# Retention and low-rank mixer on one core: batch 1's u by token and through DMA, transposing DMAs on two queues, two loads and one chunk moved

## The chip, the cores and the metric

The kernel runs on one core of a Trainium2 chip. The metric is the device time of one execution in microseconds. The kernel before takes 226.94 us (median of 3 runs, 226.93 to 226.95).

The core has five engines, each with one instruction stream that it works through in order: TensorE (PE) for matrix products into PSUM, VectorE (DVE) and ScalarE (ACT) for elementwise work and for reading PSUM, GpSimd (POOL), and SyncE (SP), which here does nothing but issue DMAs. Engines and DMAs are ordered among each other by semaphores: an instruction may wait until a semaphore has reached a count, and raises one when it is done.

## The reference

Four batches of 768 tokens; 8 heads of 64 channels make 512 channels per token.

```python
gamma = 1.0 - 2.0 ** (-5.0 - np.arange(H))
for t in range(S):                                   # retention, per batch and head
    state = gamma * state + outer(k[t], v[t])
    x[t] = (q[t] @ state) / sqrt(D)
h = x.transpose(0, 2, 1) @ U @ V                     # low rank over tokens, rank 32
u = x + h.transpose(0, 2, 1)
out = u + np.maximum(u @ w_ch1, 0.0) @ w_ch2         # 512 -> 2048 -> 512
```

## The kernel before

A batch is cut into six chunks of 128 tokens. For each chunk, POOL scales k and q by powers of gamma (`ret_k`, `ret_q` in `ret_in`, line 268, giving `kd` and `qd` in bf16), ACT casts v (`ret_v`), and then:

- `ret_T` (line 415) turns `qd` and `kd` so that channels lie on partitions. For batch 1 PE does it and DVE or ACT copies the result out of PSUM; from batch 2 on (`by_dma`) two transposing DMAs do it (`ret_T_dma`, line 277): **Tq** for q, **Tk** for k.
- `ret_S` forms the scores of a chunk, and DVE masks them (tile `a`).
- `ret_O` adds the part of the old state and the part of the scores, ACT copies the sum out of PSUM (tile `x`), and DVE masks the new state (tile `state`). The state of chunk c is read by `ret_O` of chunk c + 1.

Then `mix_P` (line 486) forms the rank-32 product P from all six x, and u comes from it in one of two ways. By channel (`mix_u`): PE turns x by products with the identity, adds V times P, and ACT or DVE copies a quarter of u, turned, out of PSUM into `uT`. By token (`mix_n`, line 526): PE forms the low-rank part of one chunk of 128 tokens, DVE adds x into `res`, ACT casts that back to bf16 into `xs`, and a transposing DMA writes it to `uT`. The six of a batch are called **T0 to T5** here. Where u was made by token, the second layer's last addition uses `res`; where not, `mlp2` adds one more product of V and P per chunk. `by_token` (line 518) says which chunks go which way: before, chunks 3 to 5 of batch 1 and all of batches 2 and 3.

The first layer, **MLP1**, has 32 blocks of work per batch (`mlp1`: 16 groups of 128 hidden channels, two halves of 384 tokens, four matmuls each). Half 0 reads chunks 0 to 2 of `uT`, half 1 chunks 3 to 5. For b > 0 the order is eight blocks of half 0, eight of half 1, then in turn. Each block fills a PSUM bank that `evict` (line 118) empties through a relu into `gT`. `evict` picks ACT or DVE by a planner's account of each engine's booked time (`Balance`, `bal.book`), when the program is built. In MLP1 of batches 1 and 2 three banks take turns (`set_banks([0, 1, 2])`, line 712), in batch 3 six. The second layer, **MLP2**, has 48 slots of two matmuls (128x512), eight per chunk of 128 tokens.

The order around this work is written out by slot: `weave` (line 590) runs the slots of MLP1 and MLP2 of batch b (0 to 31, then n1 = 32 and up) and puts the retention and the mixing of batch b + 1 between them, where the tables `at` (ret_T), `S_at`, `O_at` and `mix_at` say. So slot 10 of batch 1's MLP1 is where chunk 0 of batch 2 is turned.

All DMAs of q, k, v and out, and all transposing DMAs, are issued by SP, in the program's order. Each raises one of eight semaphores when it lands (DMAHW0 to DMAHW7 below), taken in turn over all DMAs of SP and ACT, and waits first for the earlier DMA on the same one.

Of the kernel before, what the change touches and what calls it, by code (L numbers as in the profile page):

```python
# [47 lines left out]
def kernel(  # L48
# [19 lines left out]
    NCB = DM // P  # L68
# [5 lines left out]
    bal = Balance()  # L74
# [31 lines left out]
    def mm_bank(who="main"):  # L106
        if use[who] is None:
            who = "main"
        b = use[who][n_use[who] % len(use[who])]
        n_use[who] += 1  # L110
        taken[b] = n_bank[0]
        return bank(b)

    def matmul(o, l, r, cols, **kw):
        nc.tensor.matmul(o, l, r, **kw)  # L115
        bal.mm(cols)
# [21 lines left out]
    def load_chunk(b, c, kinds="kqv"):  # L138
        t = staged.setdefault((b, c), {})
        for nm in kinds:  # L140
            load_one(t, b, c, {"k": k, "q": q, "v": v}[nm], nm + "_n")
# [26 lines left out]
    for what in ("q0", "kA", "q1", "k2", "k3", "vA", "q2", "k4", "v2", "k5", "v3", "v4", "v5"):  # L168
        src, i = {"q": q, "k": k, "v": v}[what[0]], what[1]
# [74 lines left out]
    xs, rc = {}, {}  # L244
# [8 lines left out]
    def ret_q(b, c, eng):  # L253
        qd = rmid.tile([P, H, D], bf16, tag="qd", name=f"qd_{b}_{c}", bufs=4)
        eng.tensor_tensor(qd, rc[b, c]["q_n"], Gq[:, c].unsqueeze(2).to_broadcast([P, H, D]),  # L255
                          op=ALU.mult)
        rc[b, c]["qd"] = qd
# [5 lines left out]
        rc[b, c]["vb"] = vb  # L263


    EARLY = (2, 3, 4)

    def ret_in(b, c):
        ret_k(b, c, nc.gpsimd)
        ret_q(b, c, nc.gpsimd)  # L270
        if b == 1 and c in EARLY:
            load_chunk(b + 1, c - EARLY[0])

# [3 lines left out]
    def ret_T_dma(b, c):  # L277
        r = rc[b, c]
        qkT = rmid.tile([P, 2, NP, P], bf16, tag="qkT", name=f"qkT_{b}_{c}", bufs=6)
        for i, src in ((0, r["qd"]), (1, r["kd"])):  # L280
            nc.sync.dma_start_transpose(out=qkT[:, i], in_=src.rearrange("p h d -> p (h d)"))
            r["qk"[i] + "T"] = qkT[:, i]


# [2 lines left out]
    G, V, A = nc.gpsimd, nc.vector, nc.scalar  # L287
# [196 lines left out]
    uTs, gTs, Ps = {}, {}, {}  # L484
# [12 lines left out]
    def mix_x(b, hf, c, bk=None):  # L497
        pieces[b, hf, c] = piece = (mm_bank("mix") if bk is None else bank(bk))[:, :HS]
        for jj in range(HS // P):
            j = hf * (HS // P) + jj  # L500
            matmul(piece[:, ts(jj, P)], xs[b][:, j, ts(c, P)], ident, P, start=(jj == 0),
                   stop=False, skip_group_check=True)

    def mix_h(b, hf, c):
        piece = pieces.pop((b, hf, c))
        matmul(piece, Ps[b][:, ts(c, P)], Vb[:, ts(hf, HS)], HS, start=False, stop=True,
               skip_group_check=True)
        evict(uTs[b][:, c, ts(hf, HS)], piece, HS)
# [7 lines left out]
    res = {}  # L516

    def by_token(b, j):
        return b >= 2 or (b == 1 and j >= NCK // 2)

    def res_of(b):
        if b not in res:
# [3 lines left out]
    def mix_n(b, j):  # L526
        h = mm_bank("mix")
        matmul(h, Vb[:, ts(j, P)], Ps[b], DM, start=True, stop=True)
        u = res_of(b)[:, j]
        nc.vector.tensor_tensor(u, h, xs[b][:, j], op=ALU.add)  # L530
        bal.book("V", 0.69)
        nc.scalar.activation(xs[b][:, j], u, AF.Copy)  # L532
        bal.book("A", 0.63)
        nc.sync.dma_start_transpose(out=uTs[b][:, :, ts(j, P)], in_=xs[b][:, j])


    def mlp1(b, m, hf):
# [8 lines left out]
    def mlp1_two(b, ms, hf):  # L546
        if b not in gTs:
            gTs[b] = gtp.tile([P, NM, S], bf16, tag="gT", name=f"gT_{b}")
        g = [mm_bank()[:, :HS] for _ in ms]
        for cs in ((0, 1), (2, 3)):  # L550
            for m, o in zip(ms, g):
                for c in cs:
                    matmul(o, w1b[:, c, ts(m, P)], uTs[b][:, c, ts(hf, HS)], HS, start=(c == 0),
                           stop=(c == NCB - 1))
        for m, o in zip(ms, g):
            evict(gTs[b][:, m, ts(hf, HS)], o, HS, relu=True)
# [43 lines left out]
    def put(side, i, f):  # L600
        side.setdefault(int(i), []).append(f)
# [17 lines left out]
    def mix_side(b, i, side):  # L619
        put(side, i + 2, lambda: mix_P(b))  # L620
        js = [j for j in range(NCK) if by_token(b, j)]
        for n, j in enumerate(js):
            put(side, i + 5 + n, lambda j=j: mix_n(b, j))
        if b == 1:
            for c in range(NCB):
                put(side, i + 5 + len(js) + c, lambda c=c: mix_u(b, 0, c))
        return side


# [55 lines left out]
    for b in range(B):  # L685
        nxt = b + 1 < B
        slots = mlp1_slots(b)
        n1 = len(slots)
        side = {}
        set_banks([0, 1, 2, SA, SB, OB])  # L690
        if b == 0:
            taken.update({i: n for n, i in enumerate((1, 2, 0, OB, SA, SB, TP))})
            set_banks([1, 2, 0, OB, SA, SB, TP])
            slots[:4] = [lambda: mlp1_two(0, (0, 1), 0), lambda: None,
                         lambda: mlp1_two(0, (0, 1), 1), lambda: None]
            for i, s in ((1, 2), (2, 3)):
                put(side, i, lambda s=s: load_w1(512 * s, 512))
            for s in range(4):
                put(side, 4 + s, lambda s=s: load_w2(s))
            for c, nm in ((0, "kq"), (1, "kq"), (2, "kq"), (0, "v"), (3, "kq"), (1, "v"), (4, "kq"),  # L700
                          (2, "v"), (3, "v"), (5, "kq"), (4, "v"), (5, "v")):
                put(side, 14, lambda c=c, nm=nm: load_chunk(1, c, nm))
            at, lead, mix_at = [n1 + 7 + 5 * c for c in range(NCK)], 4, n1 + 38
            S_at = {(0, 1): n1 + 14, (2, 3): n1 + 24, (4,): n1 + 30, (5,): n1 + 35}
            O_at = [n1 + i for i in (19, 22, 29, 32, 35, 38)]
        if b:

            slots = slots[:16:2] + slots[1:16:2] + slots[16:]
        if b == 1:
            slots[:2] = [lambda: mlp1_two(1, (0, 1), 0), lambda: None]  # L710
        if b and nxt:
            set_banks([0, 1, 2])
            at, lead, mix_at = [10 + 4 * c for c in range(NCK)], 5, n1 + 25
            S_at = {(0, 1): 27, (2, 3): 37, (4, 5): 47}
            O_at = [32, 35, 43, 46, 53, 56]
        if nxt:
            ret_side(b + 1, at, lead, S_at, O_at, side)
            put(side, n1, lambda: set_banks([0, 1], [2]))
            put(side, mix_at, lambda: use.update(mix=[2, SA, SB, OB]))
            mix_side(b + 1, mix_at, side)  # L720
        if b in (1, 2):
            for c, i in ((3, 0), (4, 7), (5, 15)):
                put(side, i, lambda c=c: load_chunk(b + 1, c))
        weave(slots + mlp2_slots(b), side)

# [29 lines left out]
```

## Time and profile before

| | before |
|---|---|
| median of 3 runs | 226.94 us |
| the profiled execution | 226.93 us, of which the span from first to last instruction is 225.2 us |
| ACT busy | 112.0 us (50%), 220 instructions |
| DVE busy | 85.4 us (38%), 163 instructions |
| MLP1 of batch 1, 2, 3 starts on PE at | 81.52, 131.24, 180.31 us |
| MLP2 of batch 3 ends on PE at | 222.1 us |
| transposing DMAs | 24 for q and k, 15 for u, all issued by SP |
| granted TensorE clock | 1.000 |

The rows of the profile name an engine, a line of the kernel, an operation, what it writes and reads, and how many were merged. "SPq" is SP issuing. Matmuls overlap, so a matmul row lasts longer than the distance to the next one: 128x512 rows follow each other every 0.216 us, and the four of an MLP1 block take 0.65 us. Times are microseconds from the start of the span.

### The profile page before, as it was taken

To read this page: it belongs to the slowest core of one execution; us is meant where nothing else is said; L and a number is where in the kernel's file an instruction comes from. 1 tells how busy PE (TensorE), PEld (TensorE's weight loads), DVE (VectorE), ACT (ScalarE), POOL (GpSimd) and SP (SyncE) were. 2 spreads that over 40 slices of the span, in tenths; PEclk is the share of its full clock that TensorE was granted. 3 is DMA by queue.
4 is the path that set the end of the run, shared out by engine and by line. 5 is a ranking of instruction groups with operands and counts; after the bars stand their busy time and mean duration, and the time that the engine had idled before them with its cause. 6 is when DMAs were issued, how large, how long until landed. Compare 5 with 4: busy or idle time off the path is not lost.

```text
span 225.2 us, 4288 instructions
## 1 busy us (share of the span) xinstructions
PE 219.7 (98%) x1735; PEld 124.7 (55%) x1735; DVE 85.4 (38%) x163; ACT 112.0 (50%) x220; POOL 58.9 (26%) x66
## 2 busy tenths in 40 slices
PE   7998999999999999999999999999999999999994
PEld 2466655655656466556554456565554455654454
DVE  8597630003777450034673610045674410001221
ACT  3377657751355277767133547776323467760000
POOL 6756920046643431431035103330000000000000
PEclk9999999999999999999999999999999999999999
DMA  6998999999899999989499669995311580001212
GB/s 172 243 265 181 162 189 199 198 223 226 186 232 219 234 232 206 201 168 127 101 210 243 196 134 231 174 187 97 93 49 57 131 143 0 0 3 47 88 52 95
DMA packets 100772, 34.85 MB, mean 155 GB/s; under 512 B 87152, under 2 KB 97808, under 8 KB 100752
## 3 DMA queue, kind: packets, MB, share of 16 engines
q1 hardware_dynamic: 94640, 30.29, 66.0%
q0 software_dynamic: 6112, 4.29, 13.0%
q8 instruction: 13, 0.21, 0.4%
q14 instruction: 7, 0.06, 0.1%
HBM read 27.46 MB, written 6.29 MB: 150 GB/s over the span
## 4 chain that ended last, share of the span: by engine, by line
PE 90%; DMA 3%; POOL 2%; DVE 1%; ACT 1%; SPq 0%; issue 0%; ACTq 0%
PE bk L115 88%; DMA in<-in_q_dram 3%; POOL qd L304 1%; PE bk L418 1%; ACT st L292 1%; PE bk L311 1%; DVE a L345 1%; SPq L165 0%; POOL kd L299 0%; DVE kT L294 0%; PE bk L323 0%; DVE vb L294 0%; DVE res L575 0%; ACTq L292 0%
## 5 line engine op out<-in xcount | busy, mean ns | idle before, releaser
L115 PE MATMUL bk<-w2b,gT 128*128 128x512 bf16 (+2 forms) x416 | 92.0, 363 | 0.0
L115 PE MATMUL bk<-uT,w1b 128*128 128x384 bf16 x512 | 84.3, 326 | 0.0
L120 ACT ACTIVATE gT<-bk 128x384 bf16<-128x384 f32 x123 | 60.4, 491 | 31.8 <-PE bk L115 31.8
L115 PEld LDWEIGHTS <-w1b 128*128 128x128 bf16 x512 | 49.9, 98 | 33.3 <-issue 0.2
L115 PEld LDWEIGHTS <-gT 128*128 128x128 bf16 x416 | 37.9, 98 | 37.8 <-issue 0.8
L250 POOL TENSOR_TENSOR kd<-k_n,Gk 128x512 bf16<-128x512 f32 x18 | 18.8, 1042 | 77.8 <-DMA k_n<-in_k_dram 58.7
L440 DVE TENSOR_TENSOR a<-bk,mask 128x512 bf16<-128x512 f32 x36 | 22.4, 683 | 36.0 <-PE bk L115 35.8
L575 DVE TENSOR_TENSOR res<-bk,res 128x512 f32<-128x512 f32 (+2 forms) x17 | 10.6, 626 | 44.6 <-PE bk L115 44.6
L459 ACT ACTIVATE x<-bk 128x512 bf16<-128x512 f32 x18 | 10.7, 595 | 23.3 <-PE bk L115 23.3
L255 POOL TENSOR_TENSOR qd<-q_n,Gq 128x512 bf16<-128x512 f32 x18 | 18.8, 1042 | 6.8 <-DMA qkT<-qd 3.4
L478 DVE TENSOR_TENSOR state<-bk,bmask 128x512 bf16<-128x512 f32 x15 | 10.4, 691 | 10.7 <-PE bk L115 10.7
L261 ACT ACTIVATE vb<-v_n 128x512 bf16<-128x512 f32 x18 | 10.8, 622 | 5.8 <-DMA v_n<-in_v_dram 5.8
L530 DVE TENSOR_TENSOR res<-bk,x 128x512 f32<-128x512 f32 x15 | 9.7, 685 | 8.4 <-PE bk L115 8.4
L532 ACT ACTIVATE x<-res 128x512 bf16<-128x512 f32 x15 | 9.3, 630 | 7.1 <-DVE res L530 6.9
L115 PEld LDWEIGHTS <-qkT 64*128 64x128 bf16 (+1 forms) x204 | 8.4, 95 | 7.1 <-issue 3.2
L115 PE MATMUL bk<-idle 128*128 128x512 bf16 x29 | 10.3, 499 | 1.2 <-DVE idle L179 1.2
L124 DVE COPY qkT<-bk 128x1024 bf16<-128x1024 bf16 x3 | 2.1, 691 | 23.9 <-PE bk L418 23.9
L115 PE MATMUL bk<-vb,a 128*128 128x64 bf16 (+1 forms) x208 | 10.1, 193 | 0.0
L115 PE MATMUL bk<-P_sb,Vb 128*128 128x512 bf16 x24 | 9.1, 380 | 0.0
L115 PEld LDWEIGHTS <-a 128*128 128x128 bf16 (+1 forms) x208 | 8.5, 97 | 0.7
L115 PE MATMUL bk<-vb,kd 128*128 128x128 bf16 (+1 forms) x88 | 8.2, 219 | 0.2 <-DVE vb L294 0.2
L345 DVE TENSOR_TENSOR a<-bk,mask 128x512 bf16<-128x512 f32 x12 | 7.7, 684 | 1.4 <-PE bk L115 1.4
(85 smaller groups left out, 132.0 us busy)
## 6 DMA issues: line engine op xcount, KB each, us to landing
out_dram<-res SPq DMA_DIRECT2D x23, 256.0 KB, 2.4
k_n<-in_k_dram SPq DMA_DIRECT2D x22, 256.0 KB, 5.0
v_n<-in_v_dram SPq DMA_DIRECT2D x22, 256.0 KB, 5.0
q_n<-in_q_dram SPq DMA_DIRECT2D x18, 256.0 KB, 5.1
w2b<-in_moe_w_ch_dram POOLq DMA_DIRECT2D x4, 512.0 KB, 15.0
in<-in_q_dram SPq DMA_DIRECT2D x3, 512.0 KB, 6.3
w1b<-in_moe_w_ch_dram POOLq DMA_DIRECT2D x4, 256.0 KB, 6.0
w1b<-in_moe_w_ch_dram POOLq DMA_DIRECT2D x2, 512.0 KB, 9.2
```

Source lines behind the costliest of these rows:

```text
L115: nc.tensor.matmul(o, l, r, **kw)
L120: nc.scalar.activation(o, i, AF.Relu if relu else AF.Copy)
L250: eng.tensor_tensor(kd, k_n, Gk[:, c].unsqueeze(2).to_broadcast([P, H, D]), op=ALU.mult)
L255: eng.tensor_tensor(qd, rc[b, c]["q_n"], Gq[:, c].unsqueeze(2).to_broadcast([P, H, D]), op=ALU.mult)
L261: nc.scalar.activation(vb, rc[b, c]["v_n"], AF.Copy)
L345: nc.vector.tensor_tensor(r0["a", c][:, e], r0["s", c][e].rearrange("p (n t) -> p n t", n=NP), mask0[:, c].unsqueeze(1).to_broadcast([P, N ...
L440: nc.vector.tensor_tensor(r["a"][:, e], r["s"][e].rearrange("p (n t) -> p n t", n=NP), mask4, op=ALU.mult)
L459: nc.scalar.activation(xs[b][:, c], o, AF.Copy)
L478: nc.vector.tensor_tensor(sb, ps.rearrange("p (n t) -> p n t", n=NP), bmask4, op=ALU.mult)
L530: nc.vector.tensor_tensor(u, h, xs[b][:, j], op=ALU.add)
L532: nc.scalar.activation(xs[b][:, j], u, AF.Copy)
L575: nc.vector.tensor_tensor(o, chp.pop((b, j)), o if by_token(b, j) else xs[b][:, j, ds(lo, w)], op=ALU.add)
```

## The change

Four things are changed. Batch 1's u is made by token for all six chunks, so `mix_u` is no longer called after batch 0 and three V-times-P products leave `mlp2`. The transposing DMAs alternate between two queues: Tk and the odd ones of T0 to T5 are issued by ACT (`nc.scalar`), Tq and the even ones by SP; for Tk the planner books 1.25 us of ACT. Batch 1's chunk 5 is turned one slot earlier, its scores are formed one slot earlier, `ret_O` of chunks 4 and 5 comes one and two slots earlier, `mix_at` moves from n1 + 38 to n1 + 36, and the first `mix_n` from four to five slots after that to four. And the loads of batch 2's chunk 2 move from batch 0's MLP2 to slot 0 of batch 1's MLP1 (its chunk 3 then goes to slot 2).

```diff
-    EARLY = (2, 3, 4)
+    EARLY = (2, 3)
...
         for i, src in ((0, r["qd"]), (1, r["kd"])):
-            nc.sync.dma_start_transpose(out=qkT[:, i], in_=src.rearrange("p h d -> p (h d)"))
+            (nc.scalar if i else nc.sync).dma_start_transpose(out=qkT[:, i],
+                                                              in_=src.rearrange("p h d -> p (h d)"))
+            if i:
+                bal.book("A", 1.25)
...
     def by_token(b, j):
-        return b >= 2 or (b == 1 and j >= NCK // 2)
+        return b >= 1
...
-        nc.sync.dma_start_transpose(out=uTs[b][:, :, ts(j, P)], in_=xs[b][:, j])
+        (nc.scalar if j % 2 else nc.sync).dma_start_transpose(out=uTs[b][:, :, ts(j, P)], in_=xs[b][:, j])
...
-            put(side, i + 5 + n, lambda j=j: mix_n(b, j))
-        if b == 1:
-            for c in range(NCB):
-                put(side, i + 5 + len(js) + c, lambda c=c: mix_u(b, 0, c))
+            put(side, i + (4 if b == 1 else 5) + n, lambda j=j: mix_n(b, j))
...
-            at, lead, mix_at = [n1 + 7 + 5 * c for c in range(NCK)], 4, n1 + 38
-            S_at = {(0, 1): n1 + 14, (2, 3): n1 + 24, (4,): n1 + 30, (5,): n1 + 35}
-            O_at = [n1 + i for i in (19, 22, 29, 32, 35, 38)]
+            at, lead, mix_at = [n1 + i for i in (7, 12, 17, 22, 27, 31)], 4, n1 + 36
+            S_at = {(0, 1): n1 + 14, (2, 3): n1 + 24, (4,): n1 + 30, (5,): n1 + 34}
+            O_at = [n1 + i for i in (19, 22, 29, 32, 34, 36)]
...
-        if b == 1:
-            slots[:2] = [lambda: mlp1_two(1, (0, 1), 0), lambda: None]
...
-            for c, i in ((3, 0), (4, 7), (5, 15)):
+            for c, i in ((2, 0), (3, 2), (4, 7), (5, 15)) if b == 1 else ((3, 0), (4, 7), (5, 15)):
```

The first place where instructions move is SP's stream at the end of batch 0's MLP2, where u of batch 1 is turned. In the rows, `uT_1` and `x_1` are batch 1's, `out_0` and `res_0` batch 0's, and the brackets hold the semaphores that a row waits for. Before:

```order
L578 DMA out_0_dram<-res_0_901 128x512 [waits DMAHW4_49,DVE_49]
L534 DMA_TRANSPOSE uT_1_1288<-x_1_1008 128x4x128 [waits DMAHW5_49,PE_49,Activation_49]
L534 DMA_TRANSPOSE uT_1_1288<-x_1_1008 128x4x128 [waits DMAHW6_49,Activation_49]
L534 DMA_TRANSPOSE uT_1_1288<-x_1_1008 128x4x128 [waits DMAHW7_49,Activation_49]
L578 DMA out_0_dram<-res_0_901 128x512 [waits DMAHW0_49,DVE_49]
```

The three are T3, T4 and T5; each waits for its own semaphore's earlier DMA and for ACT's cast, and for no other transposing DMA. The same place of SP after the change:

```order
L581 DMA out_0_dram<-res_0_901 128x512 [waits DMAHW1_49,DVE_49]
L537 DMA_TRANSPOSE uT_1_1276<-x_1_1008 128x4x128 [waits DMAHW2_49,PE_49,Activation_49]
L537 DMA_TRANSPOSE uT_1_1276<-x_1_1008 128x4x128 [waits DMAHW4_49,DMAHW3_49,Activation_49]
L537 DMA_TRANSPOSE uT_1_1276<-x_1_1008 128x4x128 [waits DMAHW6_49,DMAHW5_49,Activation_49]
L581 DMA out_0_dram<-res_0_901 128x512 [waits DMAHW0_49,DVE_49]
```

These are T0, T2 and T4, on semaphores 2, 4 and 6. T2 and T4 each have one wait more: T2 for semaphore 3, T4 for semaphore 5. Those are the semaphores of T1 and T3, which ACT issues. ACT's stream at that place after the change, from the casts of `mix_n` to the first evictions of MLP1:

```order
L535 ACTIVATE x_1_1008<-res_1_1285 128x512 [waits DVE_49] x2
L537 DMA_TRANSPOSE uT_1_1276<-x_1_1008 128x4x128 [waits DMAHW3_49,DMAHW2_49,Activation_49]
L535 ACTIVATE x_1_1008<-res_1_1285 128x512 [waits DVE_49] x2
L537 DMA_TRANSPOSE uT_1_1276<-x_1_1008 128x4x128 [waits DMAHW5_49,DMAHW4_49,Activation_49]
L535 ACTIVATE x_1_1008<-res_1_1285 128x512 [waits DVE_49] x2
L537 DMA_TRANSPOSE uT_1_1276<-x_1_1008 128x4x128 [waits DMAHW7_49,DMAHW6_49,Activation_49]
L120 ACTIVATE gT_1_1340<-bk1_122_1341 128x384 [waits PE_49]
L120 ACTIVATE gT_1_1340<-bk0_123_1347 128x384 [waits PE_49]
L120 ACTIVATE gT_1_1340<-bk2_124_1359 128x384 [waits PE_49]
```

T1, T3 and T5 stand between ACT's casts and ahead of ACT's first ten evictions of MLP1. T1 waits for semaphore 2 (T0), T3 for 4 (T2), T5 for 6 (T4). Taken together with SP's rows, each of T1 to T5 waits until the one before it has landed. Batches 2 and 3 have the same rows at the same place.

The third place is ACT's stream in MLP1 of batch 1 from slot 9 on, where batch 2's q and k are turned (`qkT_2_0` is chunk 0 of batch 2). Before it held evictions alone:

```order
L120 ACTIVATE gT_1_1355<-bk1_132_1424 128x384 [waits PE_49]
L120 ACTIVATE gT_1_1355<-bk0_133_1433 128x384 [waits PE_49]
L120 ACTIVATE gT_1_1355<-bk2_134_1439 128x384 [waits PE_49]
L120 ACTIVATE gT_1_1355<-bk1_135_1445 128x384 [waits PE_49]
L120 ACTIVATE gT_1_1355<-bk0_136_1455 128x384 [waits PE_49]
```

And now:

```order
L120 ACTIVATE gT_1_1340<-bk1_131_1415 128x384 [waits PE_49]
L281 DMA_TRANSPOSE qkT_2_0_1421<-kd_2_0_1377 128x4x128 [waits Pool_49]
L120 ACTIVATE gT_1_1340<-bk1_134_1436 128x384 [waits PE_49]
L120 ACTIVATE gT_1_1340<-bk0_135_1446 128x384 [waits PE_49]
L281 DMA_TRANSPOSE qkT_2_1_1452<-kd_2_1_1411 128x4x128 [waits DMAHW4_49,DMAHW3_49,Pool_49]
L120 ACTIVATE gT_1_1340<-bk0_138_1473 128x384 [waits PE_49]
L120 ACTIVATE gT_1_1340<-bk2_139_1483 128x384 [waits PE_49]
L281 DMA_TRANSPOSE qkT_2_2_1489<-kd_2_2_1442 128x4x128 [waits DMAHW7_49,DMAHW5_49,Pool_49]
L120 ACTIVATE gT_1_1340<-bk2_142_1504 128x384 [waits PE_49]
L120 ACTIVATE gT_1_1340<-bk1_143_1514 128x384 [waits PE_49]
```

Tk of each chunk stands after two evictions; the two evictions in between (bk_132 and 133, 136 and 137 and so on) are DVE's now. Tk of chunk 1 waits for semaphore 3, which is SP's Tq of chunk 0, and Tk of chunk 2 for semaphore 5, Tq of chunk 1. SP's stream has the other half:

```order
L135 DMA v_n_2_4_1397<-in_v_dram 128x8x64 [waits DMAHW2_49]
L281 DMA_TRANSPOSE qkT_2_0_1421<-qd_2_0_1379 128x4x128 [waits DMAHW3_49,DMAHW6_49,PE_49,Pool_49]
L281 DMA_TRANSPOSE qkT_2_1_1452<-qd_2_1_1413 128x4x128 [waits DMAHW4_49,DMAHW5_49,PE_49,Pool_49]
L135 DMA k_n_2_5_1461<-in_k_dram 128x8x64
L135 DMA q_n_2_5_1463<-in_q_dram 128x8x64 [waits DMAHW0_49]
L135 DMA v_n_2_5_1465<-in_v_dram 128x8x64 [waits DMAHW1_49]
L281 DMA_TRANSPOSE qkT_2_2_1489<-qd_2_2_1444 128x4x128 [waits DMAHW2_49,DMAHW7_49,PE_49,Pool_49]
L281 DMA_TRANSPOSE qkT_2_3_1520<-qd_2_3_1481 128x4x128 [waits DMAHW3_49,PE_49,Pool_49]
```

Tq of chunks 0 and 1 wait for semaphores 6 and 4, ACT's Tk of the same chunk; Tq of chunks 2 and 3 for 7 and 3 likewise. Behind chunk 3 SP issues Tq of chunk 4 with no wait for ACT; Tk of chunk 4 then waits for Tq of chunks 3 and 4, in batch 2 Tq of chunk 5 waits for Tk of chunk 4 and Tk of chunk 5 for Tq of chunk 5. In batch 3 Tq of chunks 3, 4 and 5 stand in a row, Tk of chunk 4 waits for all three and Tk of chunk 5 for none of them.

## The prediction

> **What bounds the kernel now.** I read the page first, then the chain of waits in order of time, then who waited for whom.
>
> ```profile
> span 225.2 us, 4288 instructions
> PE 219.7 (98%) x1735; PEld 124.7 (55%) x1735; DVE 85.4 (38%) x163; ACT 112.0 (50%) x220; POOL 58.9 (26%) x66
> ...
> 69.41 152.68 PE bk L115 x1114
> ...
> ACT gT L120 <- PE bk L115: 31.8, 120, 4.4
> ```
>
> PE is the bound, and the third line says how tightly: the chain's last 152.68 us are 1114 matmuls with no wait among them. Every other engine waits for PE; ACT did so 120 times before an eviction of MLP1. So matmuls taken out are a gain at their full length, and each new wait of PE is a loss at its full length. ACT's half-empty row promises little: it evicts in order, and what stops it stops PE as soon as the three banks are full.
>
> **PE work.** The end of batch 0's MLP2, on PE and DVE, where batch 1's u is made:
>
> ```profile
> 71.53 0.40 PE L115 MATMUL bk<-qkT 64*128 64x128 bf16 x8
> ...
> 73.91 0.40 PE L115 MATMUL bk<-state,qkT 128*128 128x128 bf16 x4
> ...
> 75.87 0.39 PE L115 MATMUL bk<-P_sb,Vb 128*128 128x512 bf16 x1
> ...
> 77.61 0.59 PE L115 MATMUL bk<-w2b,gT 128*128 128x512 bf16 x2
> 78.04 0.38 PE L115 MATMUL bk<-P_sb,Vb 128*128 128x512 bf16 x1
> ...
> 79.34 0.33 PE L115 MATMUL bk<-ident,x 128*128 128x128 bf16 x3
> ...
> 81.52 10.73 PE L115 MATMUL bk<-uT,w1b 128*128 128x384 bf16 x65
> ...
> 71.97 1.29 DVE L440 TENSOR_TENSOR a<-bk,mask 128x512 bf16<-128x512 f32 x2 [1.15 <-PE bk L115]
> 73.17 0.68 DVE L478 TENSOR_TENSOR state<-bk,bmask 128x512 bf16<-128x512 f32 x1
> 75.51 0.69 DVE L575 TENSOR_TENSOR res<-bk,x 128x512 f32<-128x512 f32 x1 [1.66 <-PE bk L115]
> ```
>
> From 79.34 to 81.52 stand the four `mix_u` and two slots of MLP2 (0.43 each, 78.04 - 77.61): 2.18 - 0.87 = 1.30 us that leave. Three `mix_n` products come (3 x 0.216 = 0.65) and three products in batch 1's MLP2 go (0.65), so **PE gains 1.30 us**.
>
> Chunk 5 drawn together gives some of it back. The state of chunk 4 is ready at 73.85, 2.32 after the scores began (71.53), and its reader `ret_O` stood at 73.91, 0.06 later. Now four matmuls instead of six (0.43 less) stand between, so PE waits about **0.45**; the masks and the state keep their length. Without that wait the first `mix_n` would stand where 75.87 is; with it t0 = 76.3. From t0 PE has six `mix_n`, one V-times-P product and eight slots: 7 x 0.216 + 8 x 0.433 = 4.98, so it reaches MLP1 at 81.3, against 81.52.
>
> **The transposes of u.** This decides. One transposing DMA alone, all of u's, one with another close behind it, one right behind loads, and SP's six loads ahead of that one:
>
> ```profile
> L534 SPq DMA_TRANSPOSE uT<-x x1: 1196/1196/1196, 124.0 to 124.0; - x1
> ...
> DMA to landing us min/median/max: 2.5/2.5/2.5
> ```
> ```profile
> L534 SPq EVENT_SEMAPHORE  x15: 17/17/28, 79.5 to 180.2; - x15
> L534 SPq DMA_TRANSPOSE uT<-x x15: 1196/1222/1829, 79.6 to 180.3; - x15
> ```
> ```profile
> L534 SPq DMA_TRANSPOSE uT<-x x1: 1217/1217/1217, 129.8 to 129.8; - x1
> ...
> DMA to landing us min/median/max: 3.6/3.6/3.6
> ```
> ```profile
> L281 SPq DMA_TRANSPOSE qkT<-qd x1: 1776/1776/1776, 91.0 to 91.0; - x1
> ...
> DMA to landing us min/median/max: 4.2/4.2/4.2
> ```
> ```profile
> 85.41 0.39 SPq L135 DMA_DIRECT2D k_n<-in_k_dram  x1
> ...
> 91.00 1.78 SPq L281 DMA_TRANSPOSE qkT<-qd  x1
> ```
>
> An issue takes 1.2 us of its stream and lands 2.5 us after it began when nothing is near, 3.6 with others in the queue, 4.2 behind loads. On one queue the next follows after the issue, about 1.3 us later. After the change the rows of the order show each transpose waiting for the one before it, on the other queue, to land: a **hop** of 2.5 instead of 1.3. And ACT, which works in order, stands still in each of these waits with its evictions behind it (the waits are instructions of the issuing stream: the EVENT_SEMAPHORE row).
>
> The Trainium skill has the reason (DMA: Bandwidth & Descriptors, "Silent corruption: two transposing streams in flight at once"): transposes from SP and from ACT must not be in flight together, the later stream must wait for the full completion count of the earlier. The program's waits are just that; no run here shows what happens without them. By this rule two queues cost 2.5 per transpose, by the row of one queue 1.3, and the sum would then be that of the second rival below.
>
> Batch 1: slot 39's last addition comes on DVE ahead of the first `mix_n` addition (75.51 follows its matmul by about 0.15), so two additions of 0.69 and a cast of 0.63 (row below) put T0 at t0 + 2.35 = 78.65. T2 is issued two hops later, 83.65, and lands at 86.15: MLP1's half 0 begins there, not at 81.3. T5 is issued at 78.65 + 5 x 2.5 = 91.15; its issue holds ACT to 92.4. Only then comes the first eviction (0.49, row below): 92.9. PE has three banks, so its fourth block starts at 92.95; before it was 81.52 + 3 x 0.65 = 83.47. **Batch 1's start: +9.5** (gain in PE work so far and the 0.45 are in it). SP's own queue adds nothing: with chunk 2's loads moved it has only outputs ahead of T0, and those loads, now behind T4, are needed at slot 18.
>
> Batches 2 and 3, before:
>
> ```profile
> 122.18 0.38 PE L115 MATMUL bk<-P_sb,Vb 128*128 128x512 bf16 x1
> ...
> 131.24 14.95 PE L115 MATMUL bk<-uT,w1b 128*128 128x384 bf16 x91
> ...
> 171.25 0.38 PE L115 MATMUL bk<-P_sb,Vb 128*128 128x512 bf16 x1
> ...
> 180.31 3.90 PE L115 MATMUL bk<-uT,w1b 128*128 128x384 bf16 x23
> ```
> ```profile
> 123.97 2.50 SPq L534 DMA_TRANSPOSE uT<-x  x2
> ```
> ```profile
> 172.39 0.63 ACT L532 ACTIVATE x<-res 128x512 bf16<-128x512 f32 x1 [1.71 <-DVE res L530]
> ...
> 181.16 0.49 ACT L120 ACTIVATE gT<-bk 128x384 bf16<-128x384 f32 x1 [4.07 <-PE bk L115]
> ```
>
> T0 comes 1.79 after the first `mix_n` (123.97 - 122.18), MLP1 9.06 after it. T2 lands at 1.79 + 7.5 = 9.3, hardly late. But T5 is issued at 14.3, ends at 15.5, first eviction at 16.0. Batch 2's fourth block (three banks) was at 9.06 + 1.95 = 11.0: **+5.0**. Batch 3 has six banks: its seventh block was at 9.06 + 3.9 = 12.95: **+3.05**.
>
> **The transposes of q and k.** In MLP1 of batches 1 and 2, ACT's six Tk stand four blocks apart (2.6 us); each pair Tk, Tq now takes two hops, 5.0, and ACT stands still until its turn. Two blocks in four are DVE's, three banks bridge one wait, not five. Where PE stood at `ret_O` of chunk 1 (slot 35):
>
> ```profile
> 104.95 0.39 PE L115 MATMUL bk<-state,qkT 128*128 128x128 bf16 x4
> ...
> 154.45 0.39 PE L115 MATMUL bk<-state,qkT 128*128 128x128 bf16 x4
> ```
>
> From the fourth block: 7 blocks and an eviction to Tk of chunk 0, 5.25. SP stood still in T2 and T4 as well; T4 goes out at 88.65, so its nine loads are issued from 90.5 to 99 (six took 5.6) and are still in flight at Tk of chunk 0 (92.95 + 5.25 = 98.2), so that hop is 4.2: to Tk of chunk 1 4.2 + 2.5 = 6.7; to chunk 2 5.0; to chunk 3 again 6.7, because chunk 5's loads go ahead of a Tq; to chunk 4 2.5 + 1.25 + 2.5 = 6.25; to chunk 5 5.0; then the issue 1.25, `vb` and `x` (0.62 and 0.6, below), after which `ret_O` of chunk 1 has its v and its bank: 2.5. Sum 37.4. Before: 104.95 - 83.47 = 21.5. **+15.9**. Batch 3's: 5.25 + 6.7 + 5.0 + 6.7, then three Tq in a row before Tk of chunk 4 (7.5), then 5.8 (two issues, three evictions, two `vb`, an `x`): 36.95, before 154.45 - (131.24 + 1.95) = 21.25: **+15.7**.
>
> ```profile
> L459 ACT ACTIVATE x<-bk 128x512 bf16<-128x512 f32 x18 | 10.7, 595 | 23.3 <-PE bk L115 23.3
> ...
> L261 ACT ACTIVATE vb<-v_n 128x512 bf16<-128x512 f32 x18 | 10.8, 622 | 5.8 <-DMA v_n<-in_v_dram 5.8
> ```
>
> **Sum.** 9.5 + 15.9 + 5.0 + 15.7 + 3.05, less two V-times-P products behind slot 35 (0.43): +48.7. On the profiled execution, 226.93 us (span 225.2 and 1.7 around it; the median is 226.94): **275.6 us**.
>
> **Bounds of what the trace does not show.** ACT issuing a DMA: nothing to 1.25 us (SP's row); I take SP's, the only row of this kind. At nothing, the six places where an issue ends a term fall away: -7.5. A hop beside loads: 2.5 to 4.2; I take 4.2, the row with loads ahead; at 2.5 four hops lose 1.7 each, -6.8. An idle hop: 2.5 to 3.6 (the two rows above); I take 2.5, since the waits keep them alone. Some 30 hops decide; 3.6 would hold for at most those that meet outputs or loads, which I put at two in three: 20 x 1.1, +22. A gain below nothing on a hop is excluded by the landing. All low: 261; high: 297.
>
> **Rivals.**
> - *ACT's waits do not hold its evictions* (the issue sits in a queue of its own). Then only late tiles count: batch 1's half 1 waits for T5, landed at 91.15 + 2.5 = 93.65 against 81.52 + 8 x 0.65 = 86.7: +7. With Tk of chunk 0 at the forecast's 98.2 the scores at slots 27, 37 and 47 wait 3.9, 4.2 and 2.2 more for the Tq and Tk before them, +10; batch 3's likewise, +10; u's half 1 in batches 2 and 3 waits for T5 at 14.3 + 2.5 against 9.3 + 5.2, +2.3 each. About +32, 259 us. Against it: the semaphore row belongs to the issuing stream.
> - *No chain; only the issues cost.* T2 waits for T1's 1.25 on ACT and lands at t0 + 7.35 against 4.98; three banks full, 0.5 more; Tk fits (2 x 0.49 + 1.25 = 2.2 in 2.6). +2.9 - 0.2 - 0.4: about 229. For it: two queues would be free if the waits named old DMAs. Against: the semaphores named are the other queue's last ones.
> - *Not slower: PE's 1.30 counts and no transpose is late.* 226.93 - 1.30 + 0.45 = 226.1. Its place is PE's first read of `uT` in batch 1; it decides if T2 lands by t0 + 4.98, so is issued by t0 + 2.5. But x of chunk 2 is cast at t0 + 3.6 at the earliest (T0's 2.35 and two casts). So the change would have to bring T2 out ahead of its input.
>
> **Chances.** Forecast 0.84, first rival 0.09, second 0.04, third 0.02, others 0.01. What a measurement here can tell from no change is about 0.2%. Faster 0.02, same 0.01, slower 0.97. The range, 256 to 294, holds the first rival and most of the bounds; its high end leaves out a little of the dearest hop.
>
> **What would show it.** In the changed profile: PE idle before MLP1 of batch 1 for about 5 us and again after three blocks for about 5; ACT with transposes of its own whose distances are 2.5 and multiples; evictions bunched behind them; PE near 80% of a span near 274; MLP1 of batches 1 and 2 stretched from 21 to some 37 us between the fourth block and `ret_O` of chunk 1. It is wrong if ACT evicts while a transpose of its own waits, if issues on the two queues lie closer than 2 us, or if PE's row stays near 98%.

## The result, and the profile after

| | before | after |
|---|---|---|
| median | 226.94 us (6 runs, 226.92 to 226.99) | 286.5 us (6 runs, 285.47 to 288.2) |
| ratio after to before | | 1.263, 95% interval 1.258 to 1.267 |
| profiled execution, its span | 226.93, 225.2 us | 287.13, 285.0 us |
| MLP1 of batch 1, 2, 3 starts on PE at | 81.52, 131.24, 180.31 us | 86.39, 163.31, 235.78 us |
| granted TensorE clock, mean | 1.000 | 0.910 |

The change costs 59.6 us. On the page of after, the span, the engines' busy time, and the chain that ended last, by engine and by line:

```profile
span 285.0 us, 4261 instructions
...
PE 236.5 (83%) x1700; PEld 129.6 (45%) x1719; DVE 97.4 (34%) x185; ACT 100.2 (35%) x200; POOL 59.1 (21%) x66
...
PE 53%; DMA 25%; issue 9%; SPq 5%; ACTq 3%; DVE 2%; ACT 2%; POOL 0%; POOLq 0%; DVEq 0%
PE bk L115 52%; DMA qkT<-kd 9%; DMA uT<-x 8%; DMA qkT<-qd 6%; DMA k_n<-in_k_dram 2%; SPq L135 2%; SPq L165 2%; ACTq L281 1%; ACTq L537 1%; DVE res L533 1%; ACT gT L120 1%; SPq L281 1%; PE bk L421 1%; POOL kd L302 0%; DVE res L578 0%
```

Before, the chain ended in 152.68 us of matmuls without a wait. Now a quarter of it is DMA, and the three tiles at its head, `qkT` from `kd`, `uT`, `qkT` from `qd`, are the ones that transposing DMAs write: 23% of the span. PE is idle for 285.0 - 236.5 = 48.5 us, against 5.5 before. And PE is *busier*, 236.5 against 219.7, though matmuls were taken out. That second number is the clock, which comes last in this section. Who waited for whom (total us, times, longest):

```profile
ACT gT L120 <- issue: 44.9, 8, 7.2
PE bk L115 <- ACT gT L120: 36.3, 10, 4.8
...
PE bk L115 <- DMA uT<-x: 4.9, 1, 4.9
```

ACT stood 44.9 us in front of evictions for nothing that the profile counts as an engine's work ("issue"), and PE 36.3 us for ACT's evictions. What ACT stood in is seen in its own row of the timeline (start, length, then in brackets the idle time before and its end). "ACTq" is ACT issuing a DMA:

```profile
81.25 1.29 ACTq L537 DMA_TRANSPOSE uT<-x  x1
...
86.32 1.22 ACTq L537 DMA_TRANSPOSE uT<-x  x1
...
92.74 1.21 ACTq L537 DMA_TRANSPOSE uT<-x  x1
94.00 1.26 ACT L120 ACTIVATE gT<-bk 128x384 bf16<-128x384 f32 x3 [5.26 <-issue]
...
101.55 1.21 ACTq L281 DMA_TRANSPOSE qkT<-kd  x1
...
109.57 1.21 ACTq L281 DMA_TRANSPOSE qkT<-kd  x1
...
114.63 1.21 ACTq L281 DMA_TRANSPOSE qkT<-kd  x1
...
122.70 1.21 ACTq L281 DMA_TRANSPOSE qkT<-kd  x1
123.95 0.87 ACT L120 ACTIVATE gT<-bk 128x384 bf16<-128x384 f32 x2 [7.19 <-issue]
129.88 1.21 ACTq L281 DMA_TRANSPOSE qkT<-kd  x1
```

T1, T3, T5 lie 5.07 and 6.42 apart, the Tk 8.0, 5.06, 8.07 and 7.2: two hops each. Right behind them the evictions come in twos and threes, after ACT has stood for up to 7.19 us. The same stretch on PE:

```profile
86.39 4.00 PE L115 MATMUL bk<-uT,w1b 128*128 128x384 bf16 x12 [4.91 <-DMA uT<-x]
94.54 12.82 PE L115 MATMUL bk<-uT,w1b 128*128 128x384 bf16 x64 [4.15 <-ACT gT L120]
111.37 7.82 PE L115 MATMUL bk<-uT,w1b 128*128 128x384 bf16 x32 [4.01 <-ACT gT L120]
124.49 4.00 PE L115 MATMUL bk<-uT,w1b 128*128 128x384 bf16 x12 [4.75 <-ACT gT L120]
```

Twelve matmuls are three blocks, which is three banks; then PE stands until ACT comes out of T5. Before, this was one row of 108 matmuls without a wait:

```profile
81.52 17.71 PE L115 MATMUL bk<-uT,w1b 128*128 128x384 bf16 x108
```

And those twelve last 4.00 us. The first twelve of batch 2 in after, which have no wait ahead of them, last 2.12:

```profile
163.31 2.12 PE L115 MATMUL bk<-uT,w1b 128*128 128x384 bf16 x12
```

All 512 matmuls of MLP1 in the groups of before, then of after (busy us, mean ns, idle time before them):

```profile
L115 PE MATMUL bk<-uT,w1b 128*128 128x384 bf16 x512 | 84.3, 326 | 0.0
```
```profile
L115 PE MATMUL bk<-uT,w1b 128*128 128x384 bf16 x512 | 101.7, 365 | 41.2 <-ACT gT L120 36.3
```

The same matmuls are busy 17.4 us longer, beside 41.2 us of idle time. The window of after that follows the wait for T5 gives the granted clock in the column behind the five engines' busy times, 0.50:

```profile
94.54:95.82 1.28, 1.28 (x5) 0.61 (x5) 0.00 (x0) 0.71 (x2) 0.22 (x1) 0.50 1.27 227
```

### The profile page after: what moved, and what is told of

It is laid out like the page before. It is cut to its first block, busy times and chain, and to the rows that moved or that the text cites. A ratio compares the mean times of both kernels' runs of the same rounds, so it can differ in the third digit from the quotient of the medians.

```text
span 285.0 us, 4261 instructions
## 1 busy us (share of the span) xinstructions
PE 236.5 (83%) x1700; PEld 129.6 (45%) x1719; DVE 97.4 (34%) x185; ACT 100.2 (35%) x200; POOL 59.1 (21%) x66
## 4 chain that ended last, share of the span: by engine, by line
PE 53%; DMA 25%; issue 9%; SPq 5%; ACTq 3%; DVE 2%; ACT 2%; POOL 0%; POOLq 0%; DVEq 0%
PE bk L115 52%; DMA qkT<-kd 9%; DMA uT<-x 8%; DMA qkT<-qd 6%; DMA k_n<-in_k_dram 2%; SPq L135 2%; SPq L165 2%; ACTq L281 1%; ACTq L537 1%; DVE res L533 1%; ACT gT L120 1%; SPq L281 1%; PE bk L421 1%; POOL kd L302 0%; DVE res L578 0%
## 5 line engine op out<-in xcount | busy, mean ns | idle before, releaser
L115 PE MATMUL bk<-uT,w1b 128*128 128x384 bf16 x512 | 101.7, 365 | 41.2 <-ACT gT L120 36.3
L115 PEld LDWEIGHTS <-w1b 128*128 128x128 bf16 x512 | 54.7, 107 | 87.4 <-issue 60.4
L115 PE MATMUL bk<-w2b,gT 128*128 128x512 bf16 (+2 forms) x398 | 90.7, 364 | 1.4 <-issue 0.7
L120 ACT ACTIVATE gT<-bk 128x384 bf16<-128x384 f32 x104 | 49.1, 492 | 79.3 <-issue 44.9
L122 DVE TENSOR_SCALAR gT<-bk 128x384 bf16<-128x384 f32 x24 | 13.4, 557 | 80.8 <-PE bk L115 80.4
L578 DVE TENSOR_TENSOR res<-bk,res 128x512 f32<-128x512 f32 (+2 forms) x20 | 12.7, 635 | 50.3 <-PE bk L115 50.3
L443 DVE TENSOR_TENSOR a<-bk,mask 128x512 bf16<-128x512 f32 x36 | 22.4, 683 | 2.1 <-PE bk L115 1.9
L535 ACT ACTIVATE x<-res 128x512 bf16<-128x512 f32 x18 | 10.6, 624 | 26.3 <-DVE res L533 11.3
L533 DVE TENSOR_TENSOR res<-bk,x 128x512 f32<-128x512 f32 x18 | 11.5, 685 | 6.3 <-PE bk L115 6.3
L124 DVE COPY qkT<-bk 128x1024 bf16<-128x1024 bf16 x4 | 2.8, 689 | 23.9 <-PE bk L421 23.9
```

Source lines behind the costliest of these rows:

```text
L120: nc.scalar.activation(o, i, AF.Relu if relu else AF.Copy)
L122: nc.vector.tensor_relu(o, i)
L443: nc.vector.tensor_tensor(r["a"][:, e], r["s"][e].rearrange("p (n t) -> p n t", n=NP), mask4, op=ALU.mult)
L578: nc.vector.tensor_tensor(o, chp.pop((b, j)), o if by_token(b, j) else xs[b][:, j, ds(lo, w)], op=ALU.add)
```

## The experiments

The times of each are medians beside runs of the kernel before on the same chip (227.03 to 227.11 us there). Where nothing else is said, an edit is against the kernel after.

**All transposes on SP, the rest of the change kept.**

```diff
-            (nc.scalar if i else nc.sync).dma_start_transpose(out=qkT[:, i], ...)
-            if i:
-                bal.book("A", 1.25)
+            nc.sync.dma_start_transpose(out=qkT[:, i], ...)
...
-        (nc.scalar if j % 2 else nc.sync).dma_start_transpose(out=uTs[b][:, :, ts(j, P)], in_=xs[b][:, j])
+        nc.sync.dma_start_transpose(out=uTs[b][:, :, ts(j, P)], in_=xs[b][:, j])
```

> The change with all transposing DMAs back on SP, nothing booked for them on ACT; batch 1's u by token, the drawn chunk and the moved loads stay. Theory (the 60 us come from transposes on two queues that wait for each other's landing, with ACT standing still in them): T0 to T2 follow 1.3 apart, T2 lands near 83.7 against PE's arrival at 81.3, MLP1 of batch 1 starts 2.2 late, and the nine loads ahead of the first Tq make the scores at slots 27 and 37 up to 2.5 late; minus 0.43 of PE work: 228.5 to 231. Rival (u by token with its transposes so close to MLP1 costs most by itself, whatever queue): over 235. Rival (the planner's booking that sent evictions to DVE): not to be told here from the theory.

Measured 233.15 us (232.82 to 233.72), ratio 1.026 (1.024 to 1.029). So the split makes 286.5 - 233.15 = 53 us of the loss, and what is left of the change still loses 6, above the upper end expected. The planner's booking goes out together with the split here, so its share is not shown apart; the run below that splits T0 to T5 has no booking and loses 18.9 all the same. On PE:

```profile
83.84 19.39 PE L115 MATMUL bk<-uT,w1b 128*128 128x384 bf16 x108 [2.41 <-DMA uT<-x]
...
104.26 0.40 PE L115 MATMUL bk<-qkT 64*128 64x128 bf16 x8 [0.70 <-DMA qkT<-kd]
...
113.04 0.40 PE L115 MATMUL bk<-qkT 64*128 64x128 bf16 x8 [1.40 <-DMA qkT<-kd]
```

MLP1 starts 2.3 us late although T0 to T2 now go out 1.3 apart: six chunks by token need a longer lead than three. The 108 matmuls then last 19.39 against 17.71 us, 1.7 more. The windows behind the wait say why:

```profile
83.84:85.00 1.16, 1.16 (x5) 0.59 (x6) 0.00 (x0) 0.00 (x0) 0.00 (x0) 0.59 0.54 106
...
87.60:89.00 1.40, 1.40 (x11) 0.84 (x9) 0.00 (x0) 1.01 (x3) 0.00 (x0) 1.00 0.82 228
```

The granted clock was 0.50 to 0.59 for some 3.6 us, after a gap of 2.4. Two waits for Tk add 2.1, since nine loads (chunk 2's among them now) stand ahead of the first Tq in SP's queue. 2.3 + 1.7 + 2.1 less the 0.43 of the two V-times-P products is 5.7; the span is 5.8 longer.

**The split alone, on the kernel before** (the edit is against that kernel).

```diff
-            nc.sync.dma_start_transpose(out=qkT[:, i], ...)
+            (nc.scalar if i else nc.sync).dma_start_transpose(out=qkT[:, i], ...)
+            if i:
+                bal.book("A", 1.25)
...
-        nc.sync.dma_start_transpose(out=uTs[b][:, :, ts(j, P)], ...)
+        (nc.scalar if j % 2 else nc.sync).dma_start_transpose(out=uTs[b][:, :, ts(j, P)], ...)
```

> The kernel before with the transposing DMAs split over two queues and nothing else of the change. Theory: T3, T4, T5 of batch 1 form a chain of three, and the evictions of uT and gT stand behind T5 on ACT: 8 us there, then batch 2 and 3 as in the changed kernel (21, 5, 18, 3 and 1 us as its trace shows): 280 to 286. Rival (u by token costs most by itself): under 260.

Measured 287.58 us (286.31 to 288.85), ratio 1.265 (1.259 to 1.272): all of the loss with none of the other edits, a little above the 280 to 286 expected. The 6 us that the other edits lose on one queue do not add to it. The likely reading is that PE waits for the chain of transposes there anyway; no run shows it place by place.

**Half of the split each.** First only T0 to T5 alternate (Tq and Tk on SP, nothing booked), then only Tq and Tk (T0 to T5 on SP):

```diff
-            (nc.scalar if i else nc.sync).dma_start_transpose(out=qkT[:, i], ...)
-            if i:
-                bal.book("A", 1.25)
+            nc.sync.dma_start_transpose(out=qkT[:, i], ...)
```

> The change with Tq and Tk both on SP; only T0 to T5 alternate between the queues. Theory: the three starts of MLP1 alone: 11 + 5 + 3 + 1 us as the trace of the change shows them, less 0.43: 245 to 249. If the waits between queues were harmless for u: as all on one queue, 228.5 to 231.

```diff
-        (nc.scalar if j % 2 else nc.sync).dma_start_transpose(out=uTs[b][:, :, ts(j, P)], ...)
+        nc.sync.dma_start_transpose(out=uTs[b][:, :, ts(j, P)], ...)
```

> The change with T0 to T5 all on SP; only Tk is issued by ACT. Theory: 21 and 18 us in MLP1 of batches 1 and 2 and the one-queue result for the rest: 264 to 270, and together with the run that splits u alone the two add up to the change: (this) + (u split) - (one queue) = 283 to 290. If ACT's evictions were not held by its own waits: under 250.

Measured 252.03 (251.32 to 252.73) and 271.38 us (271.17 to 271.58): 18.9 and 38.2 above the kernel with one queue. Both lie some us above what was expected. Their sum over that kernel gives 290.3 against 286.5, so the two halves overlap by about 4. The transposes of q and k make twice the loss of those of u, as the prediction's sum had it (31.6 against 17.6).

**The change, with MLP1's evictions of batches 1 to 3 on DVE.** Does the loss sit in the evictions behind ACT's waits, or in the chain itself?

```diff
-        evict(gTs[b][:, m, ts(hf, HS)], g, HS, relu=True)
+        if b:
+            nc.vector.tensor_relu(gTs[b][:, m, ts(hf, HS)], g)
+        else:
+            evict(gTs[b][:, m, ts(hf, HS)], g, HS, relu=True)
```

> The change with every eviction of MLP1 in batches 1 to 3 on VectorE, so ACT's waits hold no eviction. If what sets the pace is the chain itself (Tk of chunk 5 and the vb and x behind it on ACT, before O of chunk 1), the chain only starts earlier: about 5 us less in each of batches 1 and 2, 2.5 less at the u of batch 2, so 270 to 277. The rival, that ACT's held evictions are nearly all of the loss, expects under 245; my own rival of the prediction put the late tiles alone at 259.

Measured 286.83 us (285.97 to 289.33): no gain at all, where 270 to 277 was expected. PE's waits have moved to the chain's other customers. They have not moved to DVE, which now does all these evictions (the last row, 1.2 us):

```profile
PE bk L115 <- ACT vb L261: 19.2, 2, 12.1
PE bk L115 <- DMA uT<-x: 18.3, 5, 6.0
...
PE bk L115 <- ACT x L462: 7.5, 2, 4.3
...
PE bk L115 <- DVE gT L548: 1.2, 2, 0.9
```

And ACT's row from T5 of batch 1 to `ret_O` of batch 2, now without an eviction:

```profile
94.33 34.31 ACTq L281 DMA_TRANSPOSE qkT<-kd  x5
128.68 0.63 ACT L261 ACTIVATE vb<-v_n 128x512 bf16<-128x512 f32 x1 [39.74 <-issue]
133.76 1.21 ACTq L281 DMA_TRANSPOSE qkT<-kd  x1
```

The first Tk goes out 7 us earlier, but Tq of chunk 0 behind it only 3.3 (103.78, in after 107.04): SP has its nine loads to issue first. From there the chain needs its two hops a pair as before, `vb` of chunk 0 stands behind five Tk, `vb` of chunk 1 behind six, and `ret_O` of chunk 1 began at 136.18 (after: 137.29). So the held evictions are where the loss *appeared*, not what it depends on. What was left on ACT here, `vb` and `x`, was not moved too, so the time of the bare chain with an ACT that holds nothing stays untried.

**Two queues without alternating: T0 to T5 on ACT, Tq and Tk on SP** (the edit is against the kernel with one queue).

```diff
-        nc.sync.dma_start_transpose(out=uTs[b][:, :, ts(j, P)], ...)
+        nc.scalar.dma_start_transpose(out=uTs[b][:, :, ts(j, P)], ...)
```

> Two queues without alternating: T0 to T5 all on ACT, Tq and Tk all on SP. ACT issues six DMAs per batch and has its casts and evictions behind them, but a transpose waits for the other queue only at the change from one group to the other. If the loss comes from the alternation (each transpose waits for the landing of the one before), this costs little over one queue's 233.15: the six issues of 1.2 us on ACT end about 8 us after T0, by then PE has two of its three banks full, so 233 to 237. The rival, that ACT is the wrong engine to issue transposes at all, whatever they wait for, expects most of the 252.03 of the run that split T0 to T5: 245 or more.

Measured 239.57 us (237.25 to 240.1), ratio 1.052 (1.046 to 1.058): 6.4 above one queue, where alternating the same six of each batch cost 18.9. Alternation is most of their price, not ACT as the issuer; but more than the 0 to 4 expected is left. T2 of batch 1, and PE's start of MLP1:

```profile
L534 ACTq DMA_TRANSPOSE uT<-x x1: 1463/1463/1463, 82.6 to 82.6; - x1
...
DMA to landing us min/median/max: 5.6/5.6/5.6
```
```profile
88.30 20.07 PE L115 MATMUL bk<-uT,w1b 128*128 128x384 bf16 x108 [6.77 <-DMA q_n<-in_q_dram]
```

T2 was issued at 82.56 and landed at 88.17; on one queue it went out at 81.25 and landed at 83.71. The row names q's load, which landed within 0.03 us of T2; it is `uT` that the matmul reads. On one queue the loads of batch 2 stand behind T4 in SP's order; with the transposes on ACT nothing holds SP back, and its loads (from 82.71 on) run beside T2. Issues on ACT are 1.9 apart too, 1.2 of issue and 0.63 of cast. Against one queue, MLP1 of batch 2 starts 2.7 us late (139.73 against 137.03) and that of batch 3 6.6 (192.97 against 186.36); in batch 2 PE waits 2.33 us for an eviction on ACT.

**PE kept warm through the waits of the change.** In this kernel, and in the second of the next pair, matmuls of zeros, which nothing reads, are added in MLP1, where PE was seen idle or near it.

```diff
+        def hold(n):
+            w = bank(ST)
+            for _ in range(n):
+                nc.tensor.matmul(w, idle[:, :P], idle, start=True, stop=True)
...
+
+        for i, n in {1: ((0, 18), (3, 15), (19, 14), (27, 17), (30, 11)), 2: ((0, 18), (3, 17), (19, 6), (23, 8), (27, 16), (30, 13)), 3: ((0, 18), (6, 9))}.get(b, ()):
+            put(side, i, lambda n=n: hold(n))
```

> The change with matmuls of zeros put into PE's order where its trace shows PE idle in MLP1 (18, 15, 14, 17, 11 of them in batch 1, 18, 17, 6, 8, 16, 13 in batch 2, 18 and 9 in batch 3, 0.216 us each, all a little shorter than the gap); they add work that nothing reads. Question: how much of the 59 us is the TensorE clock, granted at 0.910 of full speed on average after the change and 1.000 before. Theory: the chain of transposes sets the pace, and the low clock counts only where PE is on the path, from the fourth block to Tk of chunk 0 (1.75 in batch 1, about 1 in batch 2) and after the last wait (1.3): granted clock back to 0.97 or more, time 281 to 284. Rival (the clock is the main cost, PE's work being 8 to 9 per cent slower over some 120 us): 272 to 277. Rival (the clock costs nothing): 286.5 or more.

Measured 288.08 us (287.94 to 288.22) at a mean clock of 0.976: the time of the rival by which the clock costs nothing. The total does not decide it, for two reasons. First, not all of the zeros stand in idle time. In batch 2 PE works without a wait from the first zeros to MLP1's fourth block:

```profile
159.59 4.05 PE L725 MATMUL bk<-idle 128*128 128x512 bf16 x18
163.47 2.11 PE L115 MATMUL bk<-uT,w1b 128*128 128x384 bf16 x12
...
169.09 7.96 PE L115 MATMUL bk<-uT,w1b 128*128 128x384 bf16 x48
```

That is 9.5 us, where the change took 6.85 (163.31 to 170.16), wait included; in batch 3 it is 9.73 (235.68 to 245.41) against 6.89 for the first six blocks. So some 5.5 us of the total are the zeros' own. Without them an estimate is 282.6, inside the theory's range. Second, the added work also changed which transposes the program chains to which: Tq of chunks 0 and 1 now go out together, Tk of chunks 1 and 2 as well. Two terms can be compared. One is PE's fourth block of batch 1 to Tk of chunk 0, which ACT issued at 99.92:

```profile
94.79 3.41 PE L115 MATMUL bk<-uT,w1b 128*128 128x384 bf16 x20 [1.33 <-ACT gT L120]
```

5.13 us here, 5.25 predicted, 7.0 in the change at half clock. So the clock makes that term's error; but Tk of chunk 1 went out at 109.30, 0.27 ahead of the change's 109.57. The 1.6 us won were gone one step later, because Tk of chunk 1 here goes out behind two Tq (issued at 105.40 and 106.72) and not one. The other is what follows the last wait, in the change and then here:

```profile
242.67 18.65 PE L115 MATMUL bk<-uT,w1b 128*128 128x384 bf16 x104 [2.82 <-ACT gT L120]
```
```profile
245.41 17.06 PE L115 MATMUL bk<-uT,w1b 128*128 128x384 bf16 x104
```

The same 104 matmuls take 1.6 us less. Both terms are won by the clock; what all of it costs in the total is not shown.

**One queue, with chunk 2's loads back in batch 0's MLP2; and the same with PE kept warm ahead of MLP1 of batch 1** (16 matmuls of zeros). The edit shown is against the kernel with one queue.

```diff
-    EARLY = (2, 3)
+    EARLY = (2, 3, 4)
...
-            for c, i in ((2, 0), (3, 2), (4, 7), (5, 15)) if b == 1 else ((3, 0), (4, 7), (5, 15)):
+            for c, i in ((3, 0), (4, 7), (5, 15)):
```

> As the one-queue run, with the loads of batch 2's chunk 2 back in batch 0's MLP2. Theory: in the one-queue run 2.1 us of waits for Tk at slots 27 and 37 come from nine loads ahead of the first Tq; with six they go. But T0 to T2 now queue behind chunk 2's loads as T3 to T5 did before (5.1 to landing): T2 lands near 85.2, PE waits 3.9 before MLP1 of batch 1, then runs at half the clock for some 3.4 us (1.7 lost): 3.7 + 1.7 - 0.43: 231.5 to 232.5, the transposes late in another place. Rival (the moved loads are the whole loss on one queue): under 229.

> The run before with 16 matmuls of zeros (3.5 us, read by nothing) where PE waits ahead of batch 1's MLP1. Theory (the clock falls to half when PE has stood idle, and the blocks behind the wait pay for it): 1.5 to 1.8 less than that run, granted clock near 1.000. Rival (the slow blocks behind the wait come from late transposes or evictions): same time.

Measured 231.01 us (230.87 to 231.5), so moving the loads cost 2.1 on one queue, and 229.93 us (229.46 to 230.19), 1.1 less, not the 1.5 to 1.8 expected. MLP1 of batch 1 in the first, then in the second:

```profile
84.18 19.20 PE L115 MATMUL bk<-uT,w1b 128*128 128x384 bf16 x108 [2.79 <-DMA uT<-x]
```
```profile
81.39 3.62 PE L722 MATMUL bk<-idle 128*128 128x512 bf16 x16
84.84 17.71 PE L115 MATMUL bk<-uT,w1b 128*128 128x384 bf16 x108
```

The zeros end 0.7 late, but the 108 matmuls then take 17.71 instead of 19.20, as long as before the change. Here the low clock has its price in the total: PE alone bounds the stretch.

**Less of it: chunk 2 alone more by token, on one queue.** Batch 1's chunks 2 to 5 go by token with T2 first, and batch 2's loads of v move behind the transposes of q and k. The edit is against the kernel before, its main lines:

```diff
-        return b >= 2 or (b == 1 and j >= NCK // 2)
+        return b >= 2 or (b == 1 and j >= 2)
...
+            for c, nm, i in ((2, "kq", 0), (3, "kq", 0), (4, "kq", 7), (5, "kq", 15), (2, "v", 23),
+                                 (3, "v", 27), (4, "v", 30), (5, "v", 30)):
...
```

> The kernel before with one chunk more, not three, of batch 1 by token: chunk 2, its transpose first, all on SP; the first mix_n one slot earlier; k and q of batch 2's chunk 2 loaded in MLP1, and v of chunks 2 to 5 behind the transposes that they held up. Theory: PE saves 0.43, T2 is issued near 78.6 with nothing ahead and lands near 81.0, when PE arrives: 226.3 to 226.8. Rival (the loads in MLP1 make the scores late as in the one-queue run): 228 or more. Rival (T2 is late by over 0.5 and the clock falls): 228.

Measured 228.59 us (227.22 to 228.95), ratio 1.005 (1.003 to 1.007): a miss. The profiled execution was the fastest of the six. In it MLP1 starts at 81.36 without a wait, 0.16 ahead of before, and loses it again at one Tk of batch 3:

```profile
156.67 0.40 PE L115 MATMUL bk<-qkT 64*128 64x128 bf16 x8 [0.36 <-DMA qkT<-kd]
```

Its span is 225.4 against 225.2. What the other five executions lose beyond that, over 1 us, no trace here shows. No kernel of this study beats the one before.

## Why the prediction was right

The forecast was 275.6, the time is 286.5. The chain of hops, its places and the sign were those that the runs show; the sizes were short by 11 us in all (span: 48.7 predicted, 59.8 measured). The range, 256 to 294, is 38 us wide, so that the time lies in it says less than the steps of the sum:

| step | predicted | measured | what was off |
|---|---|---|---|
| batch 1, fourth block of MLP1 | +9.5 | +11.07 (94.54) | T3 landed 3.9 after its issue, not 2.5 |
| batch 2, `ret_O` of chunk 1 | +15.9 | +21.27 (137.29) | the clock 1.8, two hops beside loads 1.3 and 1.4, Tk of chunk 3 to 4 0.9 |
| two V-times-P products | -0.43 | -0.44 | |
| u of batch 2, fourth block | +5.0 | +5.07 (170.16) | |
| batch 3, `ret_O` of chunk 1 | +15.7 | +18.35 (209.77) | the clock 1.2, one hop beside loads 1.3, another 0.8 too dear, behind the last Tk 0.9 |
| u of batch 3, seventh block | +3.05 | +3.14 (242.67) | |
| from there to the end | 0 | +1.34 | the clock after the last wait |

- **PE work.** PE reached MLP1 at 86.39 - 4.91 = 81.48; 81.3 was predicted. The wait for chunk 5's state was 0.33 us, not 0.45.
- **The hop.** T0 was issued at 78.61 (78.65 predicted), T2 at 83.83 (83.65), and MLP1 waited for it until 86.39 (86.15). Idle hops are 2.5: Tk of chunks 1 to 2, and 4 to 5, lie 5.06 and 4.99 apart (5.0). An issue on ACT takes 1.21 (1.25). All three were unknowns, settled by the rows of SP and ACT. (The terms that the prediction names for T0 add up to 2.16, not 2.35; measured from the first `mix_n`, at 76.36, it is 2.25.)
- **The hop beside loads** is the mis-sized term. It was put at 4.2, from the row of before with loads ahead on the *same* queue. What Tk of chunk 0 of batch 2 took in after:

```profile
L281 ACTq DMA_TRANSPOSE qkT<-kd x1: 1206/1206/1206, 101.5 to 101.5; - x1
...
DMA to landing us min/median/max: 5.4/5.4/5.4
```

  It was issued among SP's nine loads; Tk of chunk 2 (+5.4) and the T5 of batches 1 and 2 (+5.1, +5.7) were the same. Per hop that is 1.3 too little: Tk of chunk 0 to 1 took 8.0 (6.7), 2 to 3 8.07 (6.7). Tk of chunk 3 to 4 took 7.2 (6.25): Tq of chunk 3 landed 3.1 after its issue and that of chunk 4 was issued late. In batch 3 one such hop was priced too dear, Tk of chunk 0 to 1 with 5.90 (6.7), since that Tk landed 3.3 after its issue: that two errors of opposite sign met there is luck.
- **The hop with nothing near** was not always 2.5. The prediction read T4 of batch 2 before (129.8, landed 3.6 after its issue) as one with another transpose close behind it; but the transposes ahead of it had one close behind them too and landed in 2.4 to 2.5. T3 of batch 1 took 3.9 with no other DMA issued by SP or ACT near it. What was near both is in the last section.
- **The clock** is the term that was missing. The prediction took each block at 0.65 us after a wait as before it. The window at 94.54 shows 0.50 instead of 1, and fourth block to Tk of chunk 0 took 7.0 instead of 5.25; the warm kernel brought that stretch to 5.13, and the last 104 matmuls of MLP1 from 18.65 to 17.06.
- **What carried the loss.** Here the mechanism was right only in part. The prediction laid the loss on ACT standing still with its evictions behind it. That is how it looks in the change (44.9 us of ACT, 36.3 of PE), but the run with the evictions on DVE shows the same time: `ret_O` of chunk 1 needs the whole chain through `vb`, half 1 of MLP1 needs T5. The first rival (259) priced late tiles alone. Its premise, that ACT's waits hold nothing behind them, is refuted by the rows of ACT in after; its price is untested, and its sum takes Tk of chunk 0 at the forecast's 98.2, which comes from held evictions.
- **Second and third rival** fall with the first row of the table: transposes lie 2.5 apart and more, and PE's 1.30 us vanish in the wait of 4.91 for `uT`. The part without the split, which is nearest to the third rival, also loses: 233.15.

## What to carry to other kernels

Before a second queue is given to transposing DMAs, look in the order of instructions for what each of them waits for: if each names the one before it on the other queue, the rate is one landing (2.5 us here) instead of one issue (1.3), and alternating is the dearest split that was tried (18.9 us for the six of u, 6.4 with all six on ACT). Price the engine that issues them by everything that stands behind them in its stream, and check a suspected carrier of a loss by taking its work away, since the wait may only move to the next customer. Where PE stands still for some microseconds, add what the next ones may cost at half clock, and then ask whether anything but PE bounds them. And when idle time is filled to test this, see in the rows that the filling ends before the wait does.

## What was not expected of the hardware

- **A transpose beside another queue's loads.** With T0 to T5 on ACT, T2 landed 5.6 us after its issue, SP's loads beginning 0.15 us behind it on the other queue; Tk of batch 2's chunk 1 in the same kernel, with loads 1.3 us behind it on its own queue, 2.5. The Trainium skill (DMA: Bandwidth & Descriptors, "Queues, rings and completion order") says that a DMA engine goes in turn through the queues that have work for it, a packet at a time. By that rule a later load on another queue shares the engines with an earlier transpose, and on the same queue it would stand behind it; 5.6 against 2.5 agrees, though the two distances differ.
- **The clock after a short gap.** A wait of 2.41 us was followed by 0.50 to 0.59 of the clock for about 3.6 us, and one of 2.79 us made 108 matmuls 1.49 us longer. The Trainium skill (TensorE: Matmul & The Clock Gate, "Part 1: The HAM clock gate (the "warmup" mystery)") gives half rate after at least one idle window of about 3.4 us, and about 3.4 us of work until the full rate. The half rate and the warm-up agree with these rows; the gaps here were shorter than the window that it names. The length of the gap alone does not decide it: behind 2.28 us in after (189.33) and 2.56 us in the warm kernel (88.11) the granted clock was 1.00, behind 2.40 us in the warm kernel (111.09) 0.50.
- **A packet of the instruction queue.** The DMA queues while T3 of batch 1 was in flight in after (86.3 to 90.3), and while T4 of batch 2 was in before (129.8 to 133.4). Behind the name stand packets, MB and the share of the 16 DMA engines; q1 holds what SP issues, q10 what ACT issues:

```profile
q10 hardware_dynamic: 544, 0.13, 47.8%
q8 instruction: 1, 0.02, 1.5%
```
```profile
q1 hardware_dynamic: 1352, 0.33, 64.4%
q8 instruction: 1, 0.02, 1.9%
```

  Each time one packet of 16 KB went out on the queue called "instruction". In after it took 0.94 us from 87.85 on, and T3's last packets followed one at a time until 89.6. T1 of the same batch, which landed in 2.5, had no such packet beside it; the T4 of batch 1 on one queue, which landed 4.2 after its issue with nothing of SP or ACT near it but other transposes, had one. So these three long hops go with such a packet. That it is their cause is likely, but no run took it away.
